# The product of keys and values moved into a ring of five PSUM banks, its sum and scaling to GpSimd

## The chip, the cores and the metric

The kernel runs on one core of one Trainium2 chip. The metric is the device time of one execution in microseconds (us). Inside the core five engines work from queues of their own, each in order: TensorE (PE; its weight loads are listed as PEld), VectorE (DVE), ScalarE (ACT), GpSimd (POOL) and the queue that issues most transfers (SP). They wait for one another through semaphores.

## The reference

Three layers stand behind each other. The change lies in the first and in the weights of the third.

```python
# 1: linear attention with a decay, B,H,S,D = 4,8,768,48
for t in range(S):
    state = f[:, :, t, :, None] * state + k_t (outer) v_t
    y[:, :, t] = q_t @ state
# 2: gate, greedy assignment of 3072 tokens to 8 experts (384 each), relu(x@w1[e])@w2[e]
# 3: h = x @ w_in (384x2048);  g = h*clip(h+3,0,6)/6;  out = g @ w_out (2048x384)
```

The weights of the third layer arrive as 64-bit words and are rebuilt as float32 (three bit operations on DVE for each piece) and then split into a high part, rounded to what the matmul takes, and a low part, the rest.

## The kernel before, in words

`attention` works on 24 chunks of 128 time steps (6 chunks for each of 4 batches, all 8 heads at once as four pairs p with two halves s). Chunks are numbered j; three chunks make a unit u. One loop, j = -1 to 24, writes out by hand the order of every engine's instructions. An iteration holds, in PE's order:

- `tg(0)` to `tg(3)`: four groups of three transposes each of raw f, k or q of a later unit (line 85). Their PSUM tiles are evacuated by ACT (f, line 89) or DVE (k, line 102; q, line 109), followed by scans on DVE (lines 95 and 97).
- `l_mm` for chunk j-1 (line 218): output and gate logits; ACT copies the output (line 223), DVE sums the logits (line 220).
- `ya_mm`: products of q with the state (line 142) and of q with the scaled keys of chunk j+1 (line 136). The latter land in the banks `pA0` and `pA1`. ACT copies these to the tile `am` (line 168) and GpSimd masks it (line 169).
- `y_mm` (line 193): masked products times v, copied by ACT (line 194, or 195 for a batch's first chunk).
- `kv_mm` (line 204): keys times values of chunk j, the increment of the state. It isn't done for the last chunk of a batch, so there are 20.
- `kt_mm` (line 176): keys of chunk j+1 transposed, copied by ACT (line 177).

PSUM has eight banks here: five that all tiles named `pT` take in turn (`PB=5`; a sixth tile waits until the first of the five has been read), `pA0`, `pA1`, and one with constants (`pC`). The tile of `kv_mm` is the bank `pA0`, which the products of line 136 have just filled.

The state is updated in `update`: DVE adds the increment to the state in place (line 211; for a batch's first chunk one multiplication instead, line 209), GpSimd multiplies by the chunk's decay (line 212). `update` is put on a list that the next `group` call empties behind its own DVE work. The state is read by line 142 of the next iteration.

Between these, `take` draws single steps from `prep`: twelve pieces of w_in (line 922, 924, 926 on DVE, 719 on ACT, low part on GpSimd at line 720) and then the first eight of sixteen pieces of w_out (lines 922, 924, 926 on DVE, 957 on ACT, low part on DVE at line 959). The remaining eight of w_out come after attention. While j is under 20 an iteration takes one to four steps, after that eight, four steps being one piece of w_out.

Routing (DVE and PE) and the experts, bound by TensorE's matmuls, follow.

Of the kernel before, what the change touches and what calls it, by code (L numbers as in the profile page):

```python
# [10 lines left out]
F32=mybir.dt.float32; F32R=mybir.dt.float32r; BF=mybir.dt.bfloat16; I32=mybir.dt.int32; U32=mybir.dt.uint32  # L11
AF=mybir.ActivationFunctionType; OP=mybir.AluOpType; AX=mybir.AxisListType
PS=bass.MemoryType.PSUM
B,H,S,D=4,8,768,48
# [3 lines left out]
def attention(tc, q,k,v,f,wg, x_dram, lg, ident, pmin, ranges, prep, setup, spin):  # L18
    nc=tc.nc
    ctx=ExitStack()  # L20
    with ctx:
        ld=ctx.enter_context(tc.tile_pool(name="ald",bufs=2))
        cs=ctx.enter_context(tc.tile_pool(name="acs",bufs=1))
        wk=ctx.enter_context(tc.tile_pool(name="awk",bufs=2))
        ps=ctx.enter_context(tc.tile_pool(name="aps",bufs=1,space=PS))
# [171 lines left out]
        def kv_mm(j):  # L197
            u,c=divmod(j,3); first=j%6==0
            if j%6==5 or j>=NCH: return
            vr=raw['v',u]  # L200
            pk=ps.tile([128,512],F32,name="pA0")[:,:NP*D].rearrange("p (a d) -> p a d",a=NP)
            for p in range(NP):
                for s in range(2):
                    nc.tensor.matmul(pk[64*s:64*s+64,p],KT[j][:,p,s],vr[:,c,2*p+s,:D],start=True,stop=True)  # L204
            sn=St[(j+1)%2][:,:,:D]; so=St[j%2][:,:,:D]
            def update():
                pcb=PC[u][:,:,c][:,:,None].to_broadcast([128,NP,D])
                if first:
                    nc.vector.tensor_tensor(out=sn,in0=pk,in1=pcb,op=OP.mult)
                else:  # L210
                    nc.vector.tensor_add(so,so,pk)
                    nc.gpsimd.tensor_tensor(out=sn,in0=so,in1=pcb,op=OP.mult)
            late.append(update)
        def l_mm(j):
            W=2*D+8
# [9 lines left out]
        ranges=ranges(lambda: ps.tile([128,384],F32,name="pT",bufs=PB),lambda: ps.tile([128,512],F32,name="pT",bufs=PB))  # L225
# [45 lines left out]
        for j in range(-1,NCH+1):  # L271
            tu,ti=divmod(j+1,3)
            tu+=1
            g=[(tu,)+x for x in ORD[4*ti:4*ti+4]] if tu<NU else [None]*4
# [18 lines left out]
            if j>=0: kv_mm(j)  # L293
# [422 lines left out]
DM=384; F1=1024; F2=2048  # L716

def split_raw(nc, raw, hi, lo, eng_lo):
    nc.scalar.copy(hi, raw)
    eng_lo.tensor_tensor(out=lo, in0=raw, in1=hi.bitcast(F32), op=OP.subtract)  # L720
# [187 lines left out]
def gla_moe_ffn(tc,q,k,v,f_logit,moe_w_gate,moe_w1,moe_w2,moe2_w_in,moe2_w_out,out):  # L908
    nc=tc.nc
    with ExitStack() as ctx:  # L910
# [3 lines left out]
        x_dram=dr.tile([B*S,DM],F32,name="x_dram")  # L914
        ident=cs.tile([128,128],F32,name="ident"); make_identity(nc,ident)
        lg=cs.tile([128,NT,E],F32,name="lg"); pmin=cs.tile([128,NU,NP,3],F32,name="pmin")
        rwk=ctx.enter_context(tc.tile_pool(name="rwk",bufs=1))
        wih=cs.tile([128,3,F2],F32R,name="wih"); wil=cs.tile([128,3,F2],F32R,name="wil")
        def join(t,words):

            V=nc.vector; lw,hw=words[:,:,0],words[:,:,1]; u=t.bitcast(U32)
            V.tensor_scalar(u,hw,3,0x3ffffff8,op0=OP.logical_shift_left,op1=OP.bitwise_and)
            yield
            V.scalar_tensor_tensor(u,hw,0xC0000000,u,op0=OP.bitwise_and,op1=OP.bitwise_or)
            yield
            V.scalar_tensor_tensor(u,lw,29,u,op0=OP.logical_shift_right,op1=OP.bitwise_or)
        def prep_in(pool):
            got={}
            def fetch(i):
                if i>11: return  # L930
                got[i]=pool.tile([128,512,2],U32,name="pw",bufs=2)
                nc.sync.dma_start(got[i].rearrange("p c t -> p (c t)"),moe2_w_in[i//4*128:i//4*128+128,i%4*512:i%4*512+512].bitcast(U32))
            fetch(0); fetch(1)
            yield
            for i in range(12):
                yield
                m=pool.tile([128,512],F32,name="pm",bufs=2); c=slice(i%4*512,i%4*512+512)
                yield from join(m,got[i])
                fetch(i+2)
                split_raw(nc,m,wih[:,i//4,c],wil[:,i//4,c],nc.gpsimd)  # L940
        woh={}; wol={}
        def prep_out(pool,wr,g0,g1,ahead,W=DM):

            words={}
            for g in range(g0,g1): words[g]=wr.tile([128,DM,2],U32,name=f"wo{g}")
            def fetch(g):
                if g<g1: nc.sync.dma_start(words[g].rearrange("p c t -> p (c t)"),moe2_w_out[g*128:(g+1)*128,:].bitcast(U32))
            for g in range(g0,g0+ahead): fetch(g)
            yield
            for g in range(g0,g1):  # L950
                yield
                m=pool.tile([128,W],F32,name="pm",bufs=2)[:,:DM]
                yield from join(m,words[g])
                fetch(g+ahead)
                w=wr.tile([128,2,DM],F32R,name=f"wo{g}")
                woh[g],wol[g]=w[:,0],w[:,1]
                nc.scalar.copy(woh[g],m)
                yield
                nc.vector.tensor_tensor(out=wol[g],in0=m,in1=woh[g].bitcast(F32),op=OP.subtract)
        def survey(pool):  # L960

            S=DM//2; V=nc.vector
# [36 lines left out]
        def both(*gens):  # L999
            for g in gens: yield from g  # L1000
# [26 lines left out]
        rt=Routing(tc,cs,lg); rt.wk=rwk  # L1027
        rt.on_ids=lambda k: got.append(k)
        rt.on_expert=lambda k: known.append(k)
        p0=rt.phase(0)  # L1030
        wr0=ctx.enter_context(tc.tile_pool(name="wout0",bufs=1))
        with tc.tile_pool(name="prep",bufs=1) as pi:
            attention(tc,q,k,v,f_logit,moe_w_gate,x_dram,lg,ident,pmin,ranges,both(prep_in(pi),prep_out(pi,wr0,0,NOUT,3,512)),lambda: (rt.constants(),p0),rt.spin)
        wr=ctx.enter_context(tc.tile_pool(name="wout",bufs=1))
        ew=ctx.enter_context(tc.tile_pool(name="ew",bufs=1))
        ew2=ctx.enter_context(tc.tile_pool(name="ew2",bufs=1))
# [7 lines left out]
        with ExitStack() as c:  # L1044
            ex=pools(c)
            po=c.enter_context(tc.tile_pool(name="po",bufs=1))
            out_parts=prep_out(po,wr,NOUT,16,16-NOUT)
            next(out_parts); w0=None
            rt.bank=None
            for i,_ in enumerate(p0):  # L1050
                if got: break
                if known and w0 is None: w0=ex.load_weights(0); next(w0)
                ex.warm(WP[min(i,len(WP)-1)])
                for _ in range(GAP.get(i,0)): next(out_parts)
            ex.gather(0)
            for _ in range(3): next(w0)
            for _ in range(GAP['ids']): next(out_parts)
            for _ in range(4): next(w0)
            ex.warm(WARM2)
            ex.make_x0(WARM3)  # L1060
            for _ in range(W0N): next(w0)
            def all_phases():
                for _ in p0: yield
                for n in range(1,E):
                    for w in rt.phase(n):
                        for _ in range(w): yield
            ap=all_phases()
            def spread(g):
                for w in g:
                    for _ in range(w): yield  # L1070
            ahead=THIRD[0]; seen=survey(po)
            for n in range(E):
                wgen=xgen=None; gat=n+1>=E; gi=None; last=n+1>=E
                for i,_ in enumerate(ex.ffn(n)):
                    if n==0:
                        if i%2==0: next(w0,None)
                        if i>=O1 and not PAUSE1[0]<=i<PAUSE1[1] and i%3==2: next(out_parts,None)
                    if not (PAUSE if n else PAUSE0)[0]<=i<(PAUSE if n else PAUSE0)[1]:
                        if n or len(got)<2 or i>=THIRD[1]: next(ap,None)
                        elif ahead: ahead-=1; next(ap,None)  # L1080
                    if n>1 and i%12==6: next(seen,None)
                    if last: continue
                    if wgen is None and len(known)>n+1 and i>=W_SLOT: wgen=ex.load_weights(n+1); wi=i; wp=max(WPMIN,min(WPMAX,(138-i)//15))
                    if not gat and len(got)>n+1 and i>=30:
                        ex.gather(n+1); gat=True; gi=i
                    if xgen is None and gat and i>=min(max(gi+(X_LAG if n else X_LAG0),X_SLOT),122 if n else 127): xgen=spread(ex.make_x(n+1))
                    if xgen is not None: next(xgen,None)
                    if wgen is not None and (i-wi)%wp==0: next(wgen,None)
                if not last:
                    while len(got)<=n+1: next(ap)  # L1090
                    if not gat: ex.gather(n+1)
                    if wgen is None: wgen=ex.load_weights(n+1)
                    for _ in wgen: pass
                    if xgen is None: xgen=spread(ex.make_x(n+1))
                    for _ in xgen: pass
            for _ in seen: pass
# [40 lines left out]
```

## Time and profile before

| | |
|---|---|
| median of 3 runs | 842.96 us (840.99 to 844.72) |
| profiled execution | 842.33 us, its span 840.5 us, 1.83 us around it |
| granted TensorE clock, mean | 0.988 of full speed |
| PE busy over the span | 796.7 us (95%) |
| DVE busy | 560.4 us (67%) |
| ACT busy | 366.2 us (44%) |
| POOL busy | 141.3 us (17%) |

The shares are means over stages that have different limits: attention fills about the first 168 us, routing and the first expert's loading the stretch to about 200 us, and the experts the rest. The change touches attention alone.

### The profile page before, as it was taken

The numbers are of one execution on the slowest core, as the hardware profiler recorded it, in microseconds if no ns is written. First come the engines' busy times: TensorE is split into PE (matmuls) and PEld (weight loads), VectorE is DVE, ScalarE is ACT, GpSimd is POOL, SyncE is SP. The second block draws the span as 40 slices with busy tenths as digits, with TensorE's granted clock in tenths as the row PEclk, the third lists the DMA queues.
The fourth block names the chain that finished last, engine by engine and source line by source line (L and its number), as shares of the span: only waits on it lengthen the run. The fifth ranks groups of instructions, "written<-read, shape, count | busy, mean of one in ns | idle before, by whom it ended". The sixth has DMA issues, their size and how long they took to land.

```text
span 840.5 us, 16833 instructions
## 1 busy us (share of the span) xinstructions
PE 796.7 (95%) x6447; PEld 762.4 (91%) x6447; DVE 560.4 (67%) x1526; ACT 366.2 (44%) x759; POOL 141.3 (17%) x233
## 2 busy tenths in 40 slices
PE   7898999888999999999999999999999999999994
PEld 6777788777989899899999999999999999999994
DVE  7999999778688548745964776666757523642431
ACT  5666776514345325423541454154316423541431
POOL 4665653311001101010100101100300020010001
PEclk9999999969999999999999999999999999999998
DMA  8899994173013112211422232322222321321000
GB/s 222 233 244 236 221 232 128 64 244 97 1 37 114 57 39 76 85 39 57 141 72 94 67 97 91 101 66 86 89 81 85 94 85 57 115 93 45 3 1 33
DMA packets 86554, 84.56 MB, mean 101 GB/s; under 512 B 30272, under 2 KB 74432, under 8 KB 86464
## 3 DMA queue, kind: packets, MB, share of 16 engines
q1 hardware_dynamic: 83392, 73.96, 31.1%
q0 software_dynamic: 3072, 9.44, 3.5%
q8 instruction: 52, 0.85, 0.4%
q14 instruction: 38, 0.31, 0.1%
HBM read 73.94 MB, written 9.44 MB: 99 GB/s over the span
## 4 chain that ended last, share of the span: by engine, by line
PE 64%; DVE 15%; issue 12%; ACT 5%; DMA 2%; POOL 2%; SPq 0%; POOLq 0%; ACTq 0%; DVEq 0%
PE acc L723 9%; PE pF L723 9%; PE acc L725 9%; PE acc L724 9%; PE pF L724 9%; PE pF L725 9%; PE pT L85 2%; DVE ga L866 2%; PE pA L136 1%; PE pT L218 1%; DVE hl L869 1%; PE pT L193 1%; DVE S L95 1%; ACT hh L868 1%; PE pA L204 1%
## 5 line engine op out<-in xcount | busy, mean ns | idle before, releaser
L723 PE MATMUL acc<-wo,hh 128*128 128x384 f32 x384 | 133.6, 348 | 0.0
L866 DVE SCALAR_TENSOR_TENSOR ga<-ga,pF 128x384 f32<-128x384 f32 x128 | 70.8, 553 | 92.4 <-ACT ga L865 91.9
L723 PE MATMUL pF<-xh,wih 128*128 128x384 f32 x384 | 131.0, 341 | 0.0
L724 PE MATMUL pF<-xh,wil 128*128 128x384 f32 x384 | 129.4, 337 | 0.0
L725 PE MATMUL acc<-wo,hh 128*128 128x384 f32 x384 | 129.3, 337 | 0.0
L725 PE MATMUL pF<-xl,wih 128*128 128x384 f32 x384 | 129.3, 337 | 0.0
L724 PE MATMUL acc<-wo,hl 128*128 128x384 f32 x384 | 129.1, 336 | 0.1
L865 ACT ACTIVATE ga<-pF,three 128x384 f32<-128x384 f32 x128 | 74.3, 580 | 96.5 <-PE pF L725 89.8
L868 ACT CAST hh<-ga 128x384 fp32r<-128x384 f32 x128 | 65.8, 514 | 98.1 <-DVE ga L866 97.4
L869 DVE TENSOR_TENSOR hl<-ga,hh 128x384 fp32r<-128x384 f32 x128 | 71.2, 556 | 29.7 <-ACT hh L868 27.7
L900 POOL DMA_INDIRECT out_dram<-ga,q_ids x24 | 24.3, 1014 | 395.6 <-ACT ga L898 392.8
L831 ACT ACTIVATE hh<-pF 128x384 fp32r<-128x384 f32 x64 | 31.5, 492 | 130.9 <-PE pF L725 125.9
L832 DVE SCALAR_TENSOR_TENSOR hl<-pF,hh 128x384 fp32r<-128x384 f32 x64 | 35.5, 555 | 70.3 <-ACT hh L831 69.9
L723 PEld LDWEIGHTS acc<-wo,hh 128*128 128x128 f32 x384 | 72.2, 188 | 1.6 <-ACT ga L865 1.5
L724 PEld LDWEIGHTS acc<-wo,hl 128*128 128x128 f32 x384 | 72.2, 188 | 0.4 <-DVE hl L869 0.4
L724 PEld LDWEIGHTS pF<-xh,wil 128*128 128x128 f32 x384 | 72.2, 188 | 0.0
L723 PEld LDWEIGHTS pF<-xh,wih 128*128 128x128 f32 x384 | 72.1, 188 | 0.0
L725 PEld LDWEIGHTS pF<-xl,wih 128*128 128x128 f32 x384 | 72.1, 188 | 0.0
L725 PEld LDWEIGHTS acc<-wo,hh 128*128 128x128 f32 x384 | 72.0, 188 | 0.0
L723 PE MATMUL pF<-xh,w1h 128*128 128x384 f32 x192 | 66.1, 344 | 0.6 <-ACT xh L801 0.6
L723 PE MATMUL acc<-hh,w2h 128*128 128x384 f32 x192 | 65.9, 343 | 0.0
L725 PE MATMUL acc<-hl,w2h 128*128 128x384 f32 x192 | 64.6, 336 | 0.3 <-DVE hl L832 0.2
(288 smaller groups left out, 1653.1 us busy)
## 6 DMA issues: line engine op xcount, KB each, us to landing
wst<-in_moe_w_dram SPq DMA_DIRECT2D x58, 192.0 KB, 2.4
wst<-in_moe_w_dram SPq DMA_DIRECT2D x42, 256.0 KB, 2.9
pw<-in_moe_w_in_dram SPq DMA_DIRECT2D x12, 512.0 KB, 4.7
wo<-in_moe_w_out_dram SPq DMA_DIRECT2D x16, 384.0 KB, 5.5
pm<-in_moe_w_out_dram SPq DMA_DIRECT2D x32, 192.0 KB, 2.5
pm<-in_moe_w_in_dram SPq DMA_DIRECT2D x30, 192.0 KB, 2.5
v<-in_v_dram SPq DMA_DIRECT2D x24, 192.0 KB, 6.2
x_dram<-y SPq DMA_DIRECT2D x24, 192.0 KB, 4.3
```

The costliest lines, as they stand in the source:

```text
L85: nc.tensor.transpose(pt[:,:,r],x[:,r,p].rearrange("p a d -> p (a d)"),ident)
L95: V.tensor_tensor_scan(SS[u,p][:,::-1],ff[:,1:U+1][:,::-1],m1[:,p%2,::-1],1.0,op0=OP.mult,op1=OP.max)
L723: nc.tensor.matmul(out, ahi, bhi, start=start, stop=False)
L724: nc.tensor.matmul(out, alo, bhi, start=False, stop=False)
L725: nc.tensor.matmul(out, ahi, blo, start=False, stop=stop)
L831: nc.scalar.activation(hh,p,AF.Relu)
L832: s.defer(2,lambda: nc.vector.scalar_tensor_tensor(hl,p,0.0,hh.bitcast(F32),op0=OP.max,op1=OP.subtract))
L865: nc.scalar.activation(a,p,AF.Relu,bias=s.three[:,0:1])
L866: late(f,1,lambda: nc.vector.scalar_tensor_tensor(g,a,6.0,p,op0=OP.min,op1=OP.mult))
L868: late(f,1,lambda: nc.scalar.copy(gh,g))
L869: late(f,3,lambda: nc.vector.tensor_tensor(out=gl,in0=g,in1=gh.bitcast(F32),op=OP.subtract))
L900: st=nc.gpsimd.indirect_dma_start(out=s.out,out_offset=bass.IndirectOffsetOnAxis(ap=ids[:,t:t+1],axis=0),in_=o,in_offset=None)
```

## The change

The tile of `kv_mm` comes from the ring `pT` in place of `pA0`. ACT copies it to a new tile `kv` in SBUF as soon as the matmuls are done. `update` then runs on GpSimd alone: an addition of the old state (not for a batch's first chunk) and the multiplication by the decay. DVE has no part in it any more. Besides, `prep_out` gets the engine for the low parts as an argument: GpSimd for the eight pieces in attention, VectorE for the eight after it.

```diff
@@ kv_mm
-            pk=ps.tile([128,512],F32,name="pA0")[:,:NP*D].rearrange("p (a d) -> p a d",a=NP)
+            pk=ps.tile([128,512],F32,name="pT",bufs=PB)[:,:NP*D].rearrange("p (a d) -> p a d",a=NP)
...
             sn=St[(j+1)%2][:,:,:D]; so=St[j%2][:,:,:D]
+            pcb=PC[u][:,:,c][:,:,None].to_broadcast([128,NP,D])
+            kv=wk.tile([128,NP,D],F32,name="kv")
+            nc.scalar.copy(kv,pk)
             def update():
-                pcb=PC[u][:,:,c][:,:,None].to_broadcast([128,NP,D])
-                if first:
-                    nc.vector.tensor_tensor(out=sn,in0=pk,in1=pcb,op=OP.mult)
-                else:
-                    nc.vector.tensor_add(so,so,pk)
-                    nc.gpsimd.tensor_tensor(out=sn,in0=so,in1=pcb,op=OP.mult)
+                if not first: nc.gpsimd.tensor_tensor(out=kv,in0=kv,in1=so,op=OP.add)
+                nc.gpsimd.tensor_tensor(out=sn,in0=kv,in1=pcb,op=OP.mult)
             late.append(update)
@@ prep_out
-        def prep_out(pool,wr,g0,g1,ahead,W=DM):
+        def prep_out(pool,wr,g0,g1,ahead,eng,W=DM):
...
-                nc.vector.tensor_tensor(out=wol[g],in0=m,in1=woh[g].bitcast(F32),op=OP.subtract)
+                eng.tensor_tensor(out=wol[g],in0=m,in1=woh[g].bitcast(F32),op=OP.subtract)
@@ the two calls
-prep_out(pi,wr0,0,NOUT,3,512)
+prep_out(pi,wr0,0,NOUT,3,nc.gpsimd,512)
-out_parts=prep_out(po,wr,NOUT,16,16-NOUT)
+out_parts=prep_out(po,wr,NOUT,16,16-NOUT,nc.vector)
```

How the order moves is seen at three places. Lines behind `kv_mm` have a number lower by one in the changed kernel (two lower between the sum and the scaling). The first place is PE's queue in the middle of attention, an iteration's end; first as it stood, then as it stands. The tile's name tells the bank.

```order
L193 MATMUL pT<-am,v_113 64x128 x8
L204 MATMUL pA_1955<-v_113,kt 64x48 x8
L85 MATMUL pT<-ident,pmq 128x128 x3
L176 MATMUL pT<-ident,kh_118 128x128 x4
L85 MATMUL pT<-ident,pmk 128x128 x3
```

```order
L193 MATMUL pT<-am,v_113 64x128 x8
L204 MATMUL pT<-v_113,kt 64x48 x8
L85 MATMUL pT<-ident,pmq 128x128 x3
L176 MATMUL pT<-ident,kh_118 128x128 x4
L85 MATMUL pT<-ident,pmk 128x128 x3
```

No row of PE has moved; one more tile of each iteration takes its turn in the ring, so that each later tile waits for a tile one place nearer to it.

The second place is DVE's queue near the end of attention (chunks 20 and 21), where steps of w_out stand close together; the numbered `wo` tiles are two pieces as they arrived (1790, 1791) and their halves (2546, 2617).

```order
L924 SCALAR_TENSOR_TENSOR pm<-wo_1790,pm 128x384
L926 SCALAR_TENSOR_TENSOR pm<-wo_1790,pm 128x384
L959 TENSOR_TENSOR wo_2546<-pm,wo_2546 128x384
L220 TENSOR_REDUCE lg<-pT 128x8
L922 TENSOR_SCALAR pm<-wo_1791 128x384
L924 SCALAR_TENSOR_TENSOR pm<-wo_1791,pm 128x384
L211 TENSOR_TENSOR St_119<-St_119,pA_2605 128x4x48
L926 SCALAR_TENSOR_TENSOR pm<-wo_1791,pm 128x384
L959 TENSOR_TENSOR wo_2617<-pm,wo_2617 128x384
L922 TENSOR_SCALAR pm<-wo_1792 128x384
```

```order
L923 SCALAR_TENSOR_TENSOR pm<-wo_1812,pm 128x384
L925 SCALAR_TENSOR_TENSOR pm<-wo_1812,pm 128x384
L219 TENSOR_REDUCE lg<-pT 128x8
L921 TENSOR_SCALAR pm<-wo_1813 128x384
L923 SCALAR_TENSOR_TENSOR pm<-wo_1813,pm 128x384
L925 SCALAR_TENSOR_TENSOR pm<-wo_1813,pm 128x384
L921 TENSOR_SCALAR pm<-wo_1814 128x384
```

DVE loses the low parts and the addition, and the bit operations of one piece follow at once on those of the piece before.

The third place is the same stretch in GpSimd's queue, before and after.

```order
L169 AFFINE_SELECT am<-am 128x512 x2
L212 TENSOR_TENSOR St_121<-St_119,pmin 128x4x48
L1007 MEMSET q_tk 3x128
L169 AFFINE_SELECT am<-am 128x512 x2
L212 TENSOR_TENSOR St_119<-St_121,pmin 128x4x48
```

```order
L169 AFFINE_SELECT am<-am 128x512 x2
L210 TENSOR_TENSOR kv<-kv,St_119 128x192
L211 TENSOR_TENSOR St_121<-kv,pmin 128x4x48
L958 TENSOR_TENSOR wo_2653<-pm,wo_2653 128x384
L1006 MEMSET q_tk 3x128
L958 TENSOR_TENSOR wo_2677<-pm,wo_2677 128x384
L169 AFFINE_SELECT am<-am 128x512 x2
L210 TENSOR_TENSOR kv<-kv,St_121 128x192
L211 TENSOR_TENSOR St_119<-kv,pmin 128x4x48
```

The addition stands between the masks and the scaling, and the low parts stand behind or ahead of the masks.

## Rows read from the trace of the kernel before

**Rows 1.** Windows by stage: length, busy PE, PEld, DVE, ACT, POOL, clock, DMA.

```profile
38.00:114.00 76.00, 67.17 (x1132) 59.03 (x1125) 71.30 (x136) 53.16 (x118) 46.51 (x76) 1.00 0.92 235
114.00:146.00 32.00, 30.39 (x544) 27.12 (x545) 31.25 (x67) 21.74 (x50) 14.16 (x35) 1.00 0.64 156
146.00:166.00 20.00, 17.67 (x339) 15.71 (x335) 15.42 (x45) 11.35 (x27) 8.79 (x13) 1.00 0.19 61
```

**Rows 2.** Waits of PE, 38 to 166 us: total, times, longest.

```profile
PE pA L204 <- ACT am L168: 10.7, 12, 2.0
```

**Rows 3.** Timeline of one iteration, all engines: start, length, engine, line.

```profile
84.97 1.09 PE L193 MATMUL pT<-am,v 128*64 128x128 f32 x16
...
86.28 1.07 ACT L168 COPY am<-pA 128x512 f32<-128x512 f32 x2
...
86.92 0.67 PE L204 MATMUL pA<-v,kt 128*64 128x48 f32 x16 [0.86 <-ACT am L168]
...
87.71 0.35 DVE L211 TENSOR_TENSOR St<-St,pA 128x192 f32<-128x192 f32 x1
...
87.98 0.19 DVE L100 RECIPROCAL m<-pmin 128x6 f32<-128x6 f32 x1
...
88.15 0.51 POOL L212 TENSOR_TENSOR St<-St,pmin 128x192 f32<-128x192 f32 x1
...
90.30 0.33 PE L142 MATMUL pT<-qt,St 64*64 64x128 f32 x2
```

**Rows 4.** Groups by line and form, 38 to 166 us: busy us, mean ns, idle before.

```profile
L720 POOL TENSOR_TENSOR wil<-pm,wih 128x512 fp32r<-128x512 f32 x11 | 14.7, 1338 | 24.3 <-ACT wih L719 24.1
...
L194 ACT COPY yt<-pT 128x256 f32<-128x256 f32 x36 | 12.0, 399 | 0.0
...
L212 POOL TENSOR_TENSOR St<-St,pmin 128x192 f32<-128x192 f32 x15 | 8.3, 551 | 0.4 <-DVE St L211 0.3
...
L924 DVE SCALAR_TENSOR_TENSOR pm<-pw,pm 128x512 uint32<-128x512 uint32 x10 | 7.7, 771 | 0.0
L922 DVE TENSOR_SCALAR pm<-pw 128x512 uint32<-128x512 uint32 x10 | 7.5, 752 | 0.0
...
L211 DVE TENSOR_TENSOR St<-St,pA 128x192 f32<-128x192 f32 x15 | 5.2, 345 | 2.6 <-PE pA L204 2.4
L959 DVE TENSOR_TENSOR wo<-pm,wo 128x384 fp32r<-128x384 f32 x8 | 4.4, 551 | 2.4 <-ACT wo L957 2.3
```

**Rows 5.** Waits of DVE, 38 to 166 us.

```profile
DVE wo L959 <- ACT wo L957: 2.3, 4, 0.6
```

**Rows 6.** Timeline of attention's last iterations, ACT and DVE.

```profile
154.52 0.56 DVE L959 TENSOR_TENSOR wo<-pm,wo 128x384 fp32r<-128x384 f32 x1 [0.58 <-ACT wo L957]
...
157.26 0.51 ACT L957 CAST wo<-pm 128x384 fp32r<-128x384 f32 x1 [2.28 <-DVE pm L926]
...
158.04 0.59 ACT L168 COPY am<-pA 128x512 f32<-128x512 f32 x1
```

**Rows 7.** Timeline of DVE's bit operations, undisturbed and beside GpSimd.

```profile
42.73 0.66 DVE L924 SCALAR_TENSOR_TENSOR pm<-pw,pm 128x512 uint32<-128x512 uint32 x1
...
49.41 0.40 DVE L922 TENSOR_SCALAR pm<-pw 128x512 uint32<-128x512 uint32 x1
...
92.80 1.30 POOL L720 TENSOR_TENSOR wil<-pm,wih 128x512 fp32r<-128x512 f32 x1 [2.34 <-ACT wih L719]
...
92.95 1.44 DVE L922 TENSOR_SCALAR pm<-pw 128x512 uint32<-128x512 uint32 x1
```

**Rows 8.** Timeline near attention's end, GpSimd and PE: the state is awaited.

```profile
160.22 0.81 POOL L212 TENSOR_TENSOR St<-St,pmin 128x192 f32<-128x192 f32 x1
...
161.08 0.33 PE L142 MATMUL pT<-qt,St 64*64 64x128 f32 x2 [0.15 <-POOL St L212]
```

**Rows 9.** Timeline of chunk 7, PE and DVE.

```profile
74.04 0.60 PE L176 MATMUL pT<-ident,kh 128*128 128x128 f32 x4
...
74.10 0.54 DVE L102 TENSOR_TENSOR kh<-pT,S 128x384 f32<-128x384 f32 x1
```

More of the change, by code (lines that the diff above doesn't have):

```diff
@@ L1032, in gla_moe_ffn @@
         with tc.tile_pool(name="prep",bufs=1) as pi:
-            attention(tc,q,k,v,f_logit,moe_w_gate,x_dram,lg,ident,pmin,ranges,both(prep_in(pi),prep_out(pi,wr0,0,NOUT,3,512)),lambda: (rt.constants(),p0),rt.spin)
+            attention(tc,q,k,v,f_logit,moe_w_gate,x_dram,lg,ident,pmin,ranges,both(prep_in(pi),prep_out(pi,wr0,0,NOUT,3,nc.gpsimd,512)),lambda: (rt.constants(),p0),rt.spin)
         wr=ctx.enter_context(tc.tile_pool(name="wout",bufs=1))
```

## The prediction

> **What bounds the kernel now.** The change touches attention only, so I read the profile by stage first, in windows over three stretches of attention [rows 1], then the waits of each engine inside them, then single iterations of the timeline. In the windows the reader is to compare DVE with the length of the stretch: 71.3 of 76 us from 38 to 114 us, 31.25 of 32 from 114 to 146, but 15.4 of 20 after that. PE is busy nearly as long, 67.2 of 76 and 30.4 of 32, yet it has a wait of its own inside: 10.7 us in 12 waits before the kv matmuls of line 204, for ACT's copy of `am` [rows 2]. The timeline shows why [rows 3]: the products of line 193 end at 86.06, the kv matmuls need the bank `pA0`, ACT only starts to copy that bank at 86.28, and PE loses 0.86 us. So up to 146 us two engines set the pace together: DVE, which is full, and PE, which is full but for a wait that the bank causes. ACT is busy 86.3 of 128 us, POOL 69.5 of 128 (sums over [rows 1]); neither paces by load. After 146 us DVE has gaps, because there the work is a chain: bit operations on DVE, the cast on ACT, the low part on DVE (which waits 0.58 us for the cast [rows 6]), then the next piece. ACT's copy of `am` stands behind those casts in ACT's queue, and came at 158.04 only after the cast that had waited 2.28 us for DVE [rows 6]. Nothing of attention overlaps with the experts, so what attention gains I carry to the end one for one.
>
> **The change part by part.**
>
> (a) *Twenty state updates leave DVE.* One addition is 0.345 us in the mean [rows 4], but instructions on DVE overlap: the next one starts 0.27 us later (87.71 to 87.98 [rows 3]), and that is what leaving it out frees. Two updates lie before 38 us, ten from 38 to 114, four from 114 to 146, four behind that. For the last DVE had been waiting, so 19 count: 19 x 0.27 = 5.1 us.
>
> (b) *Eight low parts leave DVE.* 0.551 us each [rows 4], less the overlap of 0.08 (0.35 - 0.27) that the update shows: 0.47. Four lie between 114 and 146 us: 1.9 us. The other four each waited for ACT's cast, 2.3 us in four times [rows 5], and DVE stood idle for that: 0.58 + 0.47 = 1.05 each, 4.2 us. Together with (a) 11.2 us less on the engine that paces.
>
> (c) *GpSimd gets 20 instructions more for the states* (16 additions, and 4 first scalings that were DVE's), at 0.551 us [rows 4], nearest in shape, *and eight low parts*. Of these the nearest row is line 720, 512 wide, 1.338 us [rows 4]; by width 384/512 that is about 1.0 us. Sum 11 + 8 = 19 us, on an engine with 58 us idle in these stretches. Its own load I cost at nothing; what hides it is that idle time. But DVE suffers beside it: line 922 took 0.40 us alone and 1.44 us when GpSimd was running line 720, ending 0.29 us after that instruction did [rows 7]. Mean of ten: 0.752, and for line 924 0.771 against 0.66 alone [rows 4, 7]. Excess 10 x 0.352 + 10 x 0.111 = 4.6 us for GpSimd's 46.5 busy us in the first stretch, 0.10 per us. I take that rate for the added 19 us: -1.9 us. The bounds are 0 (all of it falls beside work that doesn't care) and the one bad row: 1.04 lost to an instruction of 1.30, 0.8 per us, 15.2 us. I stay at the mean, since it is over twenty operations.
>
> The Trainium skill, "SBUF — State Buffer", section "Who interferes with whom", says that DVE and GpSimd share a pair of ports as an exclusive lock: a DVE instruction in a two-port mode, or with two SBUF inputs against a GpSimd one that reads SBUF, makes whichever comes second wait out the first. The row of 1.44 us agrees with that. Taken as a rule for every added instruction it gives the price of the second rival below; by the mean of the rows it gives 1.9 us.
>
> (d) *The state comes later on GpSimd*: two instructions behind the masks where there was one, about 0.5 us. In the full part there is room: the state was ready at 88.66 and first used at 90.30 [rows 3]. Even if PE comes 0.86 us earlier, 0.3 us are left. Near the end there is none: at 160.22 + 0.81 the state was done and PE began at 161.08, having waited [rows 8]. Queued behind that wait on PE is the whole next iteration. Three such iterations: -1.5 us. Bounds 0 and 20 x 0.5 = 10.
>
> (e) *The kv matmuls no longer wait for `am`*: up to 10.7 us freed on PE [rows 2]. I don't add this to (a) and (b), since DVE keeps the pace up to 146 us; it is what lets PE follow DVE, and a ceiling.
>
> (f) *The ring has one tile more per iteration* with the same five banks, so each tile behind kv waits for a nearer one. For most, that one was read long before. In the iterations with j = 1, 7, 13, 19 the transposes of line 176 must now wait for DVE's line 102: at 74.04 they ran before it, and DVE ended it at 74.64 [rows 9]. What queues behind them on PE is the next transposes. 4 x 0.60 = -2.4 us. Below, 0, if DVE comes earlier by as much; above, the same for all 20: 12 us.
>
> (g) *ACT gets 20 copies* from PSUM, 192 wide; the nearest row is line 194 with 0.399 us for 256 [rows 4], so at most 8.0 us. ACT's third of idle time hides them: 0. If that cover is gone (line 177 and the rest of ACT's queue stand behind the copy), the cost is the 8.0 us.
>
> Sum: -11.2 + 1.9 + 1.5 + 2.4 = -5.4 us. The profiled execution took 842.33 us (span 840.5 and 1.83 around it), 0.63 below the median of the runs. That gives 836.9 by the profiled one and 837.6 by the median; I say **837.2**.
>
> **The rivals.**
>
> *Slots and copies pace instead (no change that counts).* With the wait of line 204 gone, PE runs into the ring: kv itself, and the tiles behind it, wait for DVE's and ACT's reads, and ACT's queue is longer by 20 copies. For it: PE and DVE are within 6% of each other in both full stretches [rows 1], and ACT stands in order behind casts that wait for DVE. Against it: DVE is the fuller of the two. Then what (a) and (b) free up to 146 us is lost but for the two early updates, and 0.5 + 3 x 0.27 + 4.2 - 1.5 - 0.9 (half of c) = 3.1 us are left: about 839.5.
>
> *GpSimd's new instructions hold up DVE (slower).* Place: lines 922 and 924, which now run while GpSimd does the low part of the piece before. Price 0.8 per us, 15.2 in place of 1.9: 842.3 - 11.2 + 15.2 + 1.5 + 2.4 = 850. It decides from (11.2 - 1.5 - 2.4) / 19 = 0.38 us lost per us added. For it: the 1.44 us row, and that a low part now starts just as the next piece's bit operations do. Against: the mean of 0.10.
>
> *Both engines are set free (more).* If (c), (d) and (f) cost nothing, PE's wait is the ceiling: 842.3 - 10.7 = 831.6.
>
> **How the numbers follow.** Forecast 0.46, slots and copies 0.32, GpSimd against DVE 0.12, both free 0.10. Half a per cent, 4.2 us, is about what a measurement of this kernel can tell from no change; the first and the last case lie below 838.7, so faster 0.56, same 0.32, slower 0.12. The range takes in the ceiling and the second case with the first two us of a slowdown and leaves out most of the slower case: 831.5 to 843.5. The forecast's own range is 833 to 838.7.
>
> **What would show it.** In the profile after: PE's wait before line 204 on `am` gone or under 2 us in attention; DVE without additions of the state and with about 10 us less work before 166 us; POOL with some 19 us more; line 921 (922 before) at a mean no more than 0.2 us higher; PE waiting on the state only in the last iterations; everything behind attention as long as it was, starting some 5 us earlier. I would be wrong if PE shows a new wait for ACT or DVE at lines 85 or 176 of about the old one's size, if 921 and 923 grow by half, or if DMA, at 0.92 of its engines' time from 38 to 114 us [rows 1], lands a raw tile too late for a faster loop.

## The result and the profile after

The changed kernel takes 849.52 us in the median of six runs (846.04 to 850.65), the kernel before 843.32 in six beside it (840.99 to 844.72): 6.2 us slower, ratio 1.0072 with a 95% interval of 1.0056 to 1.0088. The prediction said 837.2, faster. The profiled execution is the quickest of the six (846.04 us, span 844.3), so the trace shows less of the loss than the medians: its span is 3.8 us longer than before, and attention's last output copy starts at 172.63 us where it started at 168.63.

Windows over the same three stretches as in [rows 1]:

```profile
38.00:114.00 76.00, 67.41 (x1121) 58.59 (x1120) 70.26 (x124) 53.42 (x126) 53.23 (x81) 1.00 0.89 229
114.00:146.00 32.00, 29.66 (x509) 26.32 (x508) 28.35 (x58) 21.89 (x52) 21.68 (x45) 1.00 0.72 171
146.00:166.00 20.00, 15.67 (x318) 13.84 (x317) 14.78 (x30) 10.87 (x27) 14.42 (x18) 1.00 0.17 56
```

GpSimd got its work (POOL 69.5 to 89.3 us in the three). DVE lost 4.6 busy us over them, most of it from 114 to 146 us, where it was full and now has 3.65 us idle. PE, whose old wait is gone, is no busier for it (67.41 us where it was 67.17, then 29.66 and 15.67 where it was 30.39 and 17.67). What they wait for, from 38 to 166 us (total, times, longest):

```profile
PE pT L142 <- POOL St L211: 5.8, 8, 1.4
PE pT L85 <- DVE kh L102: 2.4, 3, 1.1
PE pT L176 <- DVE kh L102: 2.4, 2, 1.4
...
DVE lg L219 <- ACT y L222: 4.0, 7, 1.0
DVE qt L109 <- PE pT L85: 3.1, 5, 0.9
...
DVE kh L102 <- PE pT L85: 2.1, 5, 0.6
```

The old wait for `am` (10.7 us [rows 2]) is gone, as the change says. In its place PE waits for the state, and for the ring (lines 85 and 176 behind line 102). The groups by line and form, to be read against [rows 4]; the first two lines are of the kernel before, the others of the changed one:

```profile
L95 DVE TENSOR_TENSOR_SCAN S<-ff,m 128x384 f32<-128x384 f32 x24 | 23.1, 964 | 0.0
L97 DVE TENSOR_TENSOR_SCAN P<-pC,ff 128x384 f32<-128x384 f32 x24 | 22.7, 947 | 2.8 <-ACT ff L89 2.3
...
L95 DVE TENSOR_TENSOR_SCAN S<-ff,m 128x384 f32<-128x384 f32 x24 | 23.9, 994 | 0.0
L97 DVE TENSOR_TENSOR_SCAN P<-pC,ff 128x384 f32<-128x384 f32 x23 | 21.8, 949 | 3.3 <-ACT ff L89 2.7
...
L921 DVE TENSOR_SCALAR pm<-pw 128x512 uint32<-128x512 uint32 x10 | 9.6, 964 | 0.0
...
L211 POOL TENSOR_TENSOR St<-kv,pmin 128x192 f32<-128x192 f32 x17 | 12.8, 754 | 1.2
L210 POOL TENSOR_TENSOR kv<-kv,St 128x192 f32<-128x192 f32 x14 | 10.3, 732 | 0.4
L958 POOL TENSOR_TENSOR wo<-pm,wo 128x384 fp32r<-128x384 f32 x8 | 8.9, 1114 | 7.1 <-ACT wo L956 7.1
...
L208 ACT COPY kv<-pT 128x192 f32<-128x192 f32 x17 | 6.1, 360 | 0.0
```

Line 921 (922 before) went from 752 to 964 ns, and the state's scaling on GpSimd itself from 551 to 754. ACT's new copies are as short as thought. Three places of the timeline show what that makes of an iteration; the first is chunk 7 [rows 9], the second the iteration of [rows 3], the third the stretch of [rows 6] and [rows 8]:

```profile
74.40 0.55 DVE L102 TENSOR_TENSOR kh<-pT,S 128x384 f32<-128x384 f32 x1
...
75.00 0.66 PE L176 MATMUL pT<-ident,kh 128*128 128x128 f32 x4 [1.39 <-DVE kh L102]
...
89.10 0.94 DVE L95 TENSOR_TENSOR_SCAN S<-ff,m 128x384 f32<-128x384 f32 x1
89.22 1.22 POOL L210 TENSOR_TENSOR kv<-kv,St 128x192 f32<-128x192 f32 x1
...
89.96 0.76 DVE L921 TENSOR_SCALAR pm<-pw 128x512 uint32<-128x512 uint32 x1
...
90.51 0.58 POOL L211 TENSOR_TENSOR St<-kv,pmin 128x192 f32<-128x192 f32 x1
...
91.14 0.33 PE L142 MATMUL pT<-qt,St 64*64 64x128 f32 x2 [0.44 <-POOL St L211]
...
158.05 0.33 PE L142 MATMUL pT<-qt,St 64*64 64x128 f32 x2 [1.12 <-POOL St L211]
...
159.79 0.51 ACT L956 CAST wo<-pm 128x384 fp32r<-128x384 f32 x1 [1.80 <-DVE pm L925]
160.21 0.48 ACT L222 COPY y<-pT 128x384 f32<-128x384 f32 x1
...
160.72 0.19 DVE L219 TENSOR_REDUCE lg<-pT 128x8 f32<-128x32 f32 x1 [0.96 <-ACT y L222]
```

At 73.61 (75.00 less the wait of 1.39) PE, which no longer stops for `am`, is ready for line 176; in the kernel before it got there at 74.04 and went on. Now it stands 1.39 us in front of a ring slot that `kh` has yet to read. `kh` itself ends at 74.95 where it ended at 74.64, as much later as the rest of DVE's queue there.

At 89.22 the new addition stands beside DVE's scan and takes 1.22 us, ending 0.40 after the scan does; beside no such instruction it took 0.59 (75.53). DVE's next bit operation runs beside that addition and the scaling and takes 0.76 us. In the kernel before it read:

```profile
89.45 0.47 DVE L922 TENSOR_SCALAR pm<-pw 128x512 uint32<-128x512 uint32 x1
```

The state is ready at 91.09, where it was at 88.66; 0.94 of that the masks ahead of it are already late, the rest is the addition and the longer scaling. At 160.72 DVE waits for ACT again: not for the cast, since the low part has left DVE, but for the output copy that stands behind the same cast in ACT's queue.

The drift along attention can be read from one row of each chunk, the start of ACT's copy of the output (line 223 before, 222 here; 24 of them in each trace). The table gives, for the 4th, 13th, 19th and last chunk, how much later than in the trace of before it starts (50.0, 107.8, 145.5, 168.6 us there). Attention's start wanders by a us or more between executions, so what counts is the growth along a line.

| kernel | 4th | 13th | 19th | last |
|---|---|---|---|---|
| changed | -0.8 | +0.4 | +2.0 | +4.0 |
| e1, low parts alone on GpSimd | -1.3 | -0.8 | -0.7 | -0.7 |
| e3, kv in the ring alone | +0.4 | +1.2 | +0.8 | +1.2 |
| e6, kv in the ring, keys in `pA0` | +0.2 | +0.1 | +0.1 | +0.8 |
| e8, changed, keys in `pA0` | -1.7 | -0.6 | +1.0 | +2.5 |
| e9, no additions | -0.3 | -0.8 | -0.8 | -0.8 |
| e10, e6 without additions | -1.0 | -1.0 | -1.0 | -0.4 |
| e11, spare additions on GpSimd | -0.5 | +1.5 | +2.7 | +4.6 |
| f1, scaling on DVE | +0.5 | +3.1 | +4.1 | +6.1 |
| f3, spare memsets on GpSimd | -1.0 | -1.6 | -1.6 | -1.6 |
| g1, q's reorder on ACT | +2.3 | +3.3 | +4.8 | +6.2 |
| g2, the same on e6 | +1.9 | +0.8 | +2.3 | +3.0 |

(From 146 to 166 us the granted clock was 0.91 in e11, 0.96 in f1 and 0.98 in g1, 1.00 before and after; their last column is not compared. From 38 to 114 us it was 0.98 in e1, f1 and g1, 1.00 in the others.) The changed kernel loses 1.2, 1.6 and 2.0 us: everywhere, and fastest where pieces of w_out stand close.

### The profile page after: what moved, and what is told of

The parts are those of the page before. It is cut to its first block, busy times and chain, and to the rows that moved or that the text cites. A ratio compares the mean times of both kernels' runs of the same rounds, so it can differ in the third digit from the quotient of the medians.

```text
span 844.3 us, 16889 instructions
## 1 busy us (share of the span) xinstructions
PE 796.7 (94%) x6447; PEld 761.8 (90%) x6447; DVE 557.4 (66%) x1498; ACT 369.4 (44%) x779; POOL 165.4 (20%) x261
## 4 chain that ended last, share of the span: by engine, by line
PE 58%; DVE 17%; issue 11%; POOL 4%; DMA 4%; ACT 4%; SPq 0%; POOLq 0%; ACTq 0%; DVEq 0%
PE acc L722 9%; PE pF L722 9%; PE acc L724 9%; PE acc L723 8%; PE pF L723 8%; PE pF L724 8%; DVE ga L865 2%; DVE S L95 2%; DMA qr<-in_q_dram 1%; DVE hl L868 1%; ACT hh L867 1%; DVE pm L921 1%; POOL am L169 1%; DVE P L97 1%; DVE pm L923 1%
## 5 line engine op out<-in xcount | busy, mean ns | idle before, releaser
L788 POOL DMA_INDIRECT xg<-x_dram,q_ids x24 | 24.0, 1001 | 213.7 <-PE pF L724 111.4
```

The costliest lines, as they stand in the source:

```text
L788: nc.gpsimd.indirect_dma_start(out=xg[:,h],out_offset=None,in_=s.x,in_offset=bass.IndirectOffsetOnAxis(ap=ids[:,h:h+1],axis=0))
```

## The experiments

Three theories were formed from the trace above. Theory A: GpSimd's queue has become the chain that the state hangs on. Theory B: the ring alone did it, and the rest would have gained. Theory C: GpSimd's added work slows DVE. The expectations below name further ones (D to F, P, L and Q) where they first use them.

**The parts by themselves.** e1 has only the low parts on GpSimd, e2 only the state (with the ring), e3 only the ring, e4 the state without the ring (kv still in `pA0`), e5 the ring and the low parts.

```diff
@@ e3: the one line, DVE adds as before
-            pk=ps.tile([128,512],F32,name="pA0")[:,:NP*D]...
+            pk=ps.tile([128,512],F32,name="pT",bufs=PB)[:,:NP*D]...
@@ e1: the one line in prep_out, for the eight pieces in attention
-                nc.vector.tensor_tensor(out=wol[g],...,op=OP.subtract)
+                nc.gpsimd.tensor_tensor(out=wol[g],...,op=OP.subtract)
```

> Before, with only the eight low parts of w_out on GpSimd. Theory A (GpSimd's queue has become the chain that the state hangs on, in attention's last iterations above all): the low parts alone, about 1.0 us each ahead of or between masks and scaling, cost 0 to 2 us against before (ratio 1.000 to 1.003). Theory B (the ring of five banks makes PE wait for DVE; the rest of the change helps): the low parts off DVE gain 2 to 4 us (ratio 0.995 to 0.998). Theory C (GpSimd's added work slows DVE through the shared port): a loss of 1 to 2 us with lines 922 and 924 longer by 0.1 to 0.3 us each.

> The changed kernel with the low parts left on VectorE, so ring, copy on ACT and the state's sum on GpSimd remain. Theory A: most of the loss remains if it is the two state instructions (3 to 5 us slower than before, ratio 1.004 to 1.006), PE still waiting on the state near the end but by less than 1.1 us each. Theory B: the loss of the changed kernel is kept whole or grows (6 to 8 us, ratio 1.007 to 1.009), since the gain of the low parts is taken away. Theory C: about half the loss, 3 us.

> Before, with only the kv tile moved into the ring of five banks; DVE adds and GpSimd scales as before, no copy on ACT. Theory A: PE's wait of 10.7 us before line 204 goes and nothing is added to GpSimd, so 1 to 4 us faster than before (ratio 0.995 to 0.999). Theory B: PE waits for lines 102 and 109 of DVE instead, and for DVE's addition where the bank of kv is due again: 2 to 5 us slower (ratio 1.002 to 1.006). Theory C: no change beyond what PE's wait gives, 1 to 3 us faster.

> The state's sum on GpSimd behind a copy by ACT, the kv tile left in the bank of line 136, the low parts left on VectorE. Theory A: PE's old wait before line 204 remains and the later state is added: 3 to 6 us slower than before (ratio 1.004 to 1.007). Theory B: without the ring's waits and with 20 updates off DVE: 1 to 4 us faster than before (ratio 0.995 to 0.999). Theory C: 1 to 2 us slower.

> The kv tile in the ring and the eight low parts on GpSimd, the state's sum left on DVE. Theory D (DVE and PE with its bank wait pace together, so that freeing one alone gives nothing, as the two single runs showed): 1 to 3 us faster than before (ratio 0.996 to 0.999), less than in full because the ring's waits for line 102 remain. Theory E (PE alone paces, DVE has room): like the ring alone, 0 to 2 us slower (1.000 to 1.003). Theory F (the loop product, copy, mask, state, product paces): within 1 us of the ring alone.

| kernel | median us | ratio to before | 95% interval |
|---|---|---|---|
| e1 low parts | 842.5 | 0.9996 | 0.9985 to 1.0008 |
| e2 ring and state | 847.06 | 1.0040 | 1.0026 to 1.0053 |
| e3 ring | 844.77 | 1.0016 | 1.0005 to 1.0027 |
| e4 state, no ring | 846.68 | 1.0043 | 1.0027 to 1.0060 |
| e5 ring, low parts | 843.9 | 1.0006 | 0.9993 to 1.0018 |

The state on GpSimd is the largest part (3.6 us without the ring, by e4); the ring by itself costs 1.3 us; the low parts neither gain nor cost, where the prediction counted 4 x 1.05 + 1.9 us. Behind e2, however, they add: 1.0040 to 1.0072. The ring's price depends on the rest as well: with the state on GpSimd, e2 (ring) is no slower than e4 (no ring). None of the theories forecast all of this: A had e3 faster, B had e1 faster and e2 at 1.007 or more, C had e1 slower and e3 faster. Why e1 gains nothing stands in its waits of DVE, 38 to 166 us:

```profile
DVE St L211 <- PE pA L204: 4.3, 5, 1.9
DVE lg L220 <- ACT y L223: 4.0, 7, 1.0
```

The wait for the cast (2.3 us [rows 5]) is gone, and the one for the output copy has grown from 0.6 to 4.0 us: ACT casts first and copies the output then, so DVE stops one instruction later for the same cast.

**The ring without its cost.** e6 puts kv in the ring and, in exchange, the transposed keys of line 176 in `pA0`, which has mostly been read by then; so the ring has as many tiles as before and PE's wait for `am` is gone as well. e7 adds the low parts on GpSimd; e8 makes the swap in the changed kernel.

```diff
@@ kt_mm
-            pk=ps.tile([128,NP,128],F32,name="pT",bufs=PB)
+            pk=ps.tile([128,NP,128],F32,name="pA0")
```

> The kv tile in the ring and, for it, the tile of the transposed keys (line 176) in the bank pA0; so the ring has as many tiles per iteration as before. Everything else as before. Theory D: PE's waits go, DVE remains full: 0 to 2 us faster (ratio 0.998 to 1.000). Theory E: PE's 10 us of waits go for the most part and the time with them: 4 to 7 us faster (0.992 to 0.995). Theory F: within 1 us of before.

> As the run before it, and the eight low parts of w_out on GpSimd. Theory D: both pacers freed, 3 to 6 us faster than before (ratio 0.993 to 0.997), and at least 2 us faster than without the low parts. Theory E: within 1 us of the exchange of banks alone. Theory F: within 1 us of before.

> The changed kernel with the transposed keys in the bank pA0, so that the ring has no more tiles than before; the state's sum on GpSimd behind ACT's copy. Theory D and E: the ring's waits (about 5 us in 7 waits for line 102) go, the waits for the state stay or grow, since PE comes earlier: still 3 to 5 us slower than before (ratio 1.003 to 1.006). If the ring had been the cause: no slower than before (0.997 to 1.001). Theory F: as the changed kernel, 6 us slower (1.007).

e6: 842.65 us, 0.9994 (0.9983 to 1.0006). e7: 843.0, 0.9998 (0.9985 to 1.0012). e8: 846.03, 1.0038 (1.0023 to 1.0052). So the ring's slots cost the changed kernel about 2.9 us (1.0072 less 1.0038; by the two intervals it may be 1 to 4.7, so that it isn't clear of the 1.3 alone), and 3.2 us stay without them. And PE's 10.7 us of waiting, the prediction's ceiling, were worth nothing: in e6 PE waits for DVE's `kh` in their place, and 2.0 us still for `am`. Theory D fails on e5 and e7, which it had faster, E on e6; F, the loop of product, copy, mask and state, had all but e8 right.

```profile
PE pT L85 <- DVE kh L102: 3.9, 4, 1.4
PE pT L142 <- DVE kh L102: 2.2, 4, 1.0
PE pA L176 <- ACT am L168: 2.0, 3, 1.0
```

**DVE's work taken away, and added.** e9 drops the 16 additions of the state from DVE, e10 the same on e6; f1 gives DVE the scaling too, f4 the same on e6.

```diff
@@ e9
-                    nc.vector.tensor_add(so,so,pk)
@@ f1
-                    nc.gpsimd.tensor_tensor(out=sn,in0=so,in1=pcb,op=OP.mult)
+                    nc.vector.tensor_tensor(out=sn,in0=so,in1=pcb,op=OP.mult)
```

> Before, with DVE's sixteen additions of kv to the state left out, so that the output is not the reference's; kv is computed and not read, GpSimd scales as before. It frees 16 x 0.27 = 4.3 us on DVE and adds nothing anywhere. If DVE paces attention up to 114 us (and in the low-part runs nothing was won only because DVE waited for the output's copy instead): 2 to 4 us faster than before (ratio 0.995 to 0.998). If neither DVE nor PE paces by itself, but the loop through copy, mask and state: 0 to 1 us faster, and that by the earlier state.

> The same additions left out (again not the reference's output), with kv in the ring and the transposed keys in the bank pA0, where PE no longer waits for the masks' copy. If DVE paces with PE close behind: 3 to 6 us faster than before (ratio 0.993 to 0.996), more than without the exchange of banks. If DVE paces alone: as the run without the exchange, within 1 us. If neither: within 1 us of before.

> Before, with the scaling of the state on DVE as well, behind its addition; GpSimd has no part in the state. Theory P (GpSimd's reading instructions and DVE's two-input ones shut one another out, and GpSimd's chain of masks and scaling paces DVE's scan): DVE's added 16 x 0.3 us = 5 us is paid back by a scan that no longer waits; 1 us faster to 2 us slower than before (ratio 0.999 to 1.002). Theory L (DVE's load paces): 4 to 6 us slower (1.005 to 1.007). Theory Q (the length of GpSimd's queue paces): 2 to 4 us faster (0.995 to 0.998).

> The state wholly on DVE, kv in the ring and the transposed keys in the bank pA0. Theory P: neither PE's wait for the copy nor the scan's wait for GpSimd is left, 1 to 4 us faster than before (ratio 0.995 to 0.999). Theory L: 3 to 5 us slower (1.004 to 1.006). Theory Q: 3 to 5 us faster.

e9: 842.4 us, 0.9987 (0.9970 to 1.0004). e10: 842.86, 0.9995 (0.9983 to 1.0008). f1: 846.95, 1.0053 (1.0034 to 1.0072). f4: 846.86, 1.0046 (1.0030 to 1.0061). Sixteen operations less gain 1.1 us (e9) or 0.4 (e10), neither clear of none, where 4.3 us were freed; sixteen more cost 4.5 us, 0.28 each (3.9 without PE's bank wait). So theory L holds for work added and not for work taken away; P and Q, which had f1 and f4 faster or nearly the same, fail. In the table e9 runs at exactly the pace of before from the 13th chunk to the last. Its timeline, DVE in the iteration of [rows 3]:

```profile
86.81 0.20 DVE L100 RECIPROCAL m<-pmin 128x6 f32<-128x6 f32 x1
87.30 0.56 DVE L109 TENSOR_TENSOR qt<-pT,P 128x384 f32<-128x384 f32 x1 [0.30 <-PE pT L85]
87.78 0.95 DVE L95 TENSOR_TENSOR_SCAN S<-ff,m 128x384 f32<-128x384 f32 x1
```

The 0.27 us that the addition left free become 0.30 us of waiting for the transposes that stand on PE behind kv and its wait for the bank. With that wait gone too (e10), DVE and GpSimd read:

```profile
87.31 0.52 DVE L109 TENSOR_TENSOR qt<-pT,P 128x384 f32<-128x384 f32 x1
...
87.72 0.51 POOL L211 TENSOR_TENSOR St<-St,pmin 128x192 f32<-128x192 f32 x1
87.75 1.30 DVE L95 TENSOR_TENSOR_SCAN S<-ff,m 128x384 f32<-128x384 f32 x1
```

Now DVE comes without a wait, and its scan, 0.95 us in e9, takes 1.30 beside GpSimd's scaling: the time is lost a third way. This is one iteration; where the rest of the 4.3 us goes wasn't followed row by row.

**GpSimd's work, by itself.** e11 adds to the kernel before, behind each scaling, an addition on GpSimd that nobody reads; f3 a memset of 128 x 512 there instead.

```diff
@@ e11
+                    nc.gpsimd.tensor_tensor(out=wk.tile([128,NP,D],F32,name="kv"),in0=sn,in1=so,op=OP.add)
@@ f3
+                    nc.gpsimd.memset(wk.tile([128,512],F32,name="kv"),0.0)
```

> Before, with a spare addition of the state's size on GpSimd behind each scaling, whose result nobody reads: GpSimd's load and its use of the shared port as in the changed kernel, but not ahead of the state that PE waits for. If the price of the state on GpSimd is DVE's contention: 2 to 4 us slower than before (ratio 1.002 to 1.005), line 922 longer by 0.1 to 0.2 us. If it is the later state alone: 0 to 1 us slower (1.000 to 1.001).

> Before, with a spare memset of 128x512 on GpSimd behind each scaling, about 0.5 us, as long as the spare addition is when it is not held up, but reading nothing. Theory P: DVE's scan and the bit operations with two inputs don't mind it; 0 to 1 us slower than before (ratio 1.000 to 1.001). Theory Q: 3 to 5 us slower, as the spare addition (1.004 to 1.006).

e11: 847.23 us, 1.0053 (1.0039 to 1.0067). f3: 842.06, 0.9993 (0.9980 to 1.0005). Groups by line and form, e11 and then f3:

```profile
L923 DVE TENSOR_SCALAR pm<-pw 128x512 uint32<-128x512 uint32 x10 | 9.7, 968 | 0.0
L213 POOL TENSOR_TENSOR kv<-St,St 128x192 f32<-128x192 f32 x14 | 12.9, 923 | 1.1
```

```profile
L923 DVE TENSOR_SCALAR pm<-pw 128x512 uint32<-128x512 uint32 x10 | 7.7, 771 | 0.0
L213 POOL MEMSET kv<- 128x512 f32 x15 | 7.8, 522 | 0.0
```

The same stretch of work, from the 4th output copy to the 19th, as windows of the kernel before, e11 and f3 (length, busy PE, PEld, DVE, ACT, POOL, clock, DMA):

```profile
50.03:145.49 95.46, 86.73 (x1503) 76.57 (x1501) 91.33 (x179) 65.73 (x145) 52.64 (x95) 1.00 0.83 213
49.49:148.15 98.66, 87.21 (x1503) 76.59 (x1501) 94.61 (x180) 65.76 (x146) 60.12 (x105) 1.00 0.78 204
49.03:143.88 94.85, 86.72 (x1503) 76.59 (x1501) 90.73 (x179) 65.65 (x145) 54.27 (x104) 1.00 0.82 212
```

And one pair at the same place of w_out, e11 first, then f3:

```profile
157.31 0.60 POOL L213 TENSOR_TENSOR kv<-St,St 128x192 f32<-128x192 f32 x1
157.44 0.88 DVE L960 TENSOR_TENSOR wo<-pm,wo 128x384 fp32r<-128x384 f32 x1 [0.58 <-ACT wo L958]
...
159.35 0.53 POOL L213 MEMSET kv<- 128x512 f32 x1
159.61 0.56 DVE L960 TENSOR_TENSOR wo<-pm,wo 128x384 fp32r<-128x384 f32 x1 [0.58 <-ACT wo L958]
```

An addition that nobody waits for costs 4.5 us (16 times 0.28) and lengthens DVE's bit operation from 752 to 968 ns; a memset of half a microsecond in the same place leaves it at 771 and costs nothing. In the windows e11 is 3.2 us longer than before with the same work on PE and ACT and none added to DVE, and DVE is busy 3.3 us longer. PE waits no more for the state than before (0.3 us from 38 to 166 us, where it was 0.4). So it is not GpSimd's queue that is short, nor the state that comes late: what GpSimd reads holds DVE up, and theory C has its cause, though it costs more than the 2 to 4 us that the expectation of e11 gave it. Theory Q, by which the memset would have cost as much, fails again; P had f3 right. The Trainium skill, "SBUF — State Buffer", section "Who interferes with whom", says that a DVE instruction with two SBUF inputs contends with a GpSimd one that reads SBUF and not with one that only writes it. The pair above agrees (line 960 has two such inputs), and so do the scans: line 97, one of whose inputs is in PSUM, took 947 ns before and 949 in the changed kernel, line 95, with both in SBUF, 964 and 994. Line 922, which lost most, reads one tensor only, so that sentence doesn't cover it; that it is held up is what the rows show.

**Attempts to buy the contention back.** e12 starts each piece's line 922 ahead of the last bit operation of the piece before, so that it misses GpSimd's low part; f2 does so with three raw buffers. g1 gives the reorder of q (line 70) of all units but the first to ACT, which takes its reads off GpSimd (21 operations, not the 18 that the expectation counts); g2 does this on e6.

```diff
@@ e12, prep_in (begin(i): a new pm, and the first bit operation of piece i)
             for i in range(12):
-                m=...; yield from join(m,got[i])
+                ...; next(j)
+                nx=begin(i+1) if i<11 else None
+                next(j,None)
                 fetch(i+2)
                 split_raw(nc,m,wih[:,i//4,c],wil[:,i//4,c],nc.gpsimd)
@@ g1, reorder
+            elif u>0: nc.scalar.copy(o,x)
```

> Before, with the first bit operation of each piece of w_in (line 922) taken ahead of the last one of the piece before it, so that it no longer stands right behind the start of that piece's low part on GpSimd. If DVE paces up to 114 us and is held up there by GpSimd: line 922 falls from 0.75 to 0.4 to 0.5 us in the mean, and the kernel is 1 to 3 us faster (ratio 0.996 to 0.999). If the delay only moves to line 924, or DVE doesn't pace: within 1 us of before.

> The earlier run with line 922 ahead of the last bit operation of the piece before, now with three buffers for the raw words, each fetched one piece earlier. If the loss of that run was its 17 us of waits for these transfers: they go, line 922 stays near 0.45 to 0.5 us, and it is 3 us faster to 1 us slower than before (ratio 0.996 to 1.001). If the later casts were the loss: 3 to 8 us slower (1.004 to 1.01).

> The kernel before with the reorder of q (line 70) of every unit but the first on ScalarE instead of GpSimd: 18 operations that read and write SBUF leave GpSimd and join ScalarE. If what holds VectorE up is GpSimd's reading through the port that both use, the reverse of the additions that nobody read is to be seen: the lines of the low parts and of the narrowing get shorter and the kernel is 1 to 3 us faster (ratio 0.996 to 0.999). If ScalarE's queue paces as closely as VectorE does, its 18 copies of about half a microsecond (9 us) come back as waits for kh, ff or y, and the kernel is 1 to 4 us slower (1.001 to 1.005).

> The same edit on the kernel with kv in the ring and the transposed keys in pA0, where TensorE no longer waits for pA0's eviction. If VectorE, through GpSimd's reads, is the only pace left, 1 to 4 us faster than before (0.995 to 0.999), and more than without the swap. If ScalarE paces, as without the swap, 1 to 4 us slower (1.001 to 1.005).

e12: 856.12 us, 1.0158 (1.0139 to 1.0178). f2: 843.03, 1.0007 (0.9994 to 1.0021). g1: 847.46, 1.0064 (1.0045 to 1.0084). g2: 845.3, 1.0041 (1.0027 to 1.0056). In e12 the operation did get short, but the raw tile is now held longer and the next one fetched too late; the group of line 922:

```profile
L922 DVE TENSOR_SCALAR pm<-pw 128x512 uint32<-128x512 uint32 x10 | 4.9, 486 | 19.7 <-DMA pw<-in_moe_w_in_dram 17.3 <-POOL am L169 2.5
```

With the third buffer (f2) the transfer wait is gone and nothing is gained. The delay has only moved: line 922 stays short (485 ns), but line 924 now stands beside the low part or the scaling and takes 924 ns where it took 771, and the scan of line 95 takes 1081 where it took 964:

```profile
L95 DVE TENSOR_TENSOR_SCAN S<-ff,m 128x384 f32<-128x384 f32 x24 | 26.0, 1081 | 0.0
...
L924 DVE SCALAR_TENSOR_TENSOR pm<-pw,pm 128x512 uint32<-128x512 uint32 x10 | 9.2, 924 | 0.0
```

In g1 the bit operations got shorter, as the contention would have it, and DVE waits for ACT instead, at line 98 (97 before):

```profile
L98 DVE TENSOR_TENSOR_SCAN P<-pC,ff 128x384 f32<-128x384 f32 x24 | 22.8, 952 | 7.8 <-ACT ff L90 7.4
...
L923 DVE TENSOR_SCALAR pm<-pw 128x512 uint32<-128x512 uint32 x10 | 6.6, 662 | 0.0
```

ACT, with a third of its time idle, is the next that paces: the wait for `ff` was 2.3 us. g2 gains most on the kernel before along a stretch (in the table 1.9 to 0.8 from the 4th to the 13th chunk, -1.1 us in 58, where e6 has -0.1, e9 -0.5 and f3 -0.6); it begins late and loses again later. Whether moving only the units in that stretch would beat the kernel before wasn't tried. No version here beat it.

## Why the prediction was wrong

The forecast failed, and its second rival, GpSimd against DVE, is what happened in kind: slower, and in large part because DVE is held up. That it gave 850 (chance 0.12) and 849.5 was measured is luck: its sum has a gain of 11.2 us that wasn't there and a price of 15.2 that was some 10 us too high (by the estimate under (c)).

**(a) and (b), the 11.2 us freed on DVE, are the step that failed.** The work left, but it was no gain: e9 measures the additions at 1.1 us (0.9987; interval 2.5 to -0.3), e1 the low parts at 0.3. This is the largest error: with (c) at its measured price and the 11.2 us left in, the sum would still say faster, by 1.7 us (estimate: -11.2 + 5.6 + 1.5 + 2.4). The prediction took an engine busy 71.3 of 76 us for the pace and PE, 6% behind, for one that follows. In the iteration shown from e9 the two lie within 0.3 us of each other, so that the 0.27 us taken from DVE are given to a wait for PE; near the end e1 shows the same with ACT's copy behind its cast. Its own sentence on PE (full but for a wait that the bank causes) held the warning: a wait of 0.86 us on PE ahead of the transposes that DVE waits for is part of DVE's loop.

**(c), 1.9 us for GpSimd beside DVE, was mis-sized.** e11's additions cost 4.5 us. Their time on GpSimd was 14.8 us (16 times 923 ns), held up as they were; at the 0.551 us of a quiet row, by which the prediction counted, it is 8.8. So the price is 0.51 per us counted so, against the assumed 0.10, and about 5.6 us for the 20 state instructions (estimate); e1 shows none for the eight low parts. In the changed kernel itself the rows that stayed on DVE got 4.1 us longer from 38 to 166 us (estimate from the groups' means: line 921 3.5, line 95 0.7, line 925 0.6, line 923 0.8 less). The mean of 0.10 was taken from all of GpSimd's time before, most of it masks and reorders, and only from two lines of DVE. The rival's 0.8, from one row, was too high.

**(d), the state's lateness, 1.5 us:** PE waits 5.8 us for it in eight times, longest 1.4. These aren't only the last iterations, as the prediction said: at 91.14 PE waits 0.44 us, where the step had left 0.3 us of room. The step reckoned two instructions at 0.551; they take 732 and 754 ns in the mean, since GpSimd is held up as well. How much of the 5.8 us is lost twice with the low parts isn't settled: e2, without these on GpSimd, has 4.2 us of that wait and 1.0040.

**(e), PE's wait as a ceiling:** it went, as said, and bought nothing (e6, 0.9994). **(f), the ring, 2.4 us** for line 176 behind line 102: the place was right, though line 85 waits there too. The waits are longer than the 0.60 us counted, since PE comes earlier; the ring alone makes them just as long, as e3 shows in chunk 7:

```profile
75.33 0.66 PE L176 MATMUL pT<-ident,kh 128*128 128x128 f32 x4 [1.39 <-DVE kh L102]
```

What they cost is less than their sum: 1.3 us alone (e3), about 2.9 in the whole change (against e8). **(g), ACT's copies at nothing:** 17 at 360 ns; nothing was measured on them apart, and g1 shows that 17 longer ones (512 ns) are not free.

Theory B fell: without the ring's cost the change still loses 3.2 us (e8). That the gains weren't there is shown by e9, e1 and e6, and that GpSimd's reads are paid by DVE by e11 with f3. What the late state (theory A) costs beyond that no run measures apart. The parts don't add up exactly: e1, e3 and e4 sum to 4.6 us, the whole is 6.2, and which wait makes the difference stays open.

Of the prediction's signs, the old wait gone and GpSimd's 19 us more came (19.9). DVE's work fell by 4.6 us and not about 10, since its other rows got longer, and line 921's mean rose by 0.21 us, just over the 0.2 allowed. Lines 85 and 176 wait 4.8 us for `kh`, about half of the old wait.

## What to carry to other kernels

An engine's busy share, even 94%, hinted here at what more work on it would cost (f1), not at what less would gain, and part of busy time is time in which an instruction is held up. So follow one iteration, take the work away in thought, and look for the next wait within the time it frees. Work given to an idle GpSimd is paid by DVE when it reads SBUF beside DVE's bit operations and scans over SBUF, as here; a price per microsecond has to be taken from operations of that kind. A tile added to a ring makes each later tile wait for a nearer reader, and an engine that the same change sets free comes to that wait earlier.

## What the runs showed of the hardware

The contention runs both ways and shows on each pair of lines: GpSimd's product of 128 x 192 took 551 ns before, 754 in the changed kernel, and the added sum up to 1.22 us; DVE's scan with two SBUF inputs 0.95 us in e9 and 1.30 in e10, where the same scan with one input in PSUM stayed at 943 to 952 ns in the mean in every kernel here. DVE's low part of w_out took 0.88 us beside an addition on GpSimd and 0.56 beside a memset. A memset of 128 x 512 on GpSimd (522 ns, 15 of them in the stretch) left DVE's lines as they were (line 95 at 961 ns, line 922 at 771).
